# A convolution and gated MLP on one core: output product in 256-column tasks, another order of first products, convolution items also in odd steps' outputs

## Chip, cores, metric

One core of one Trainium2 chip. The metric is the device time of one execution in microseconds, median of several runs; the kernel before takes 2473.99 us (three runs, 2473.96 to 2475.25). "TensorE" is the matmul engine (PE in the profile, PEld for its weight loads), "DVE" is VectorE, "ACT" is ScalarE.

## The reference

```python
# x (8, 4096, 192), weight (8, 7), w_in (192, 2048), w_out (2048, 192), all float32
w = softmax(weight, axis=-1)                       # per head, 7 taps
x_pad = concatenate([zeros((8, 6, 192)), x], axis=1)
conv[b, s, h, :] = sum_k w[h, k] * x_pad[b, s + k, h, :]     # 8 heads of 24 channels
t = conv.reshape(32768, 192)
h = t @ w_in                                       # first product
g = h * sigmoid(1.702 * h)
out = g @ w_out                                    # second product
```

## The kernel before

Tokens go through in 64 steps (s = 0 to 63) of 512, and both products of a step are computed as 2x2 block products with seven multiplications each instead of eight (P1 to P7), so that sums and differences of blocks are made on DVE and fewer matmuls are left for TensorE. A step has the first product in two units (`a` and `b`, half of the hidden columns each), then `output`, the second product. Convolution and loads for later tokens are cut into 31 small items per two steps, queued in `todo`; `work(n)` runs n of them at that place of DVE's program. The output part and the steady step:

```python
LANES = [(0, 0, 0, TA, 0), (1, 0, TA, T - TA, 0), (2, 1, T // 2, T // 2, 0),
         (3, 2, T - TA, TA, 0), (1, 1, 0, T // 2, T - TA), (2, 2, 0, T - TA, T // 2)]
# T = 256, TA = 192: three 32-row chunks of 256 tokens dealt to four strips of 192 columns

def product2(slot, bank, a, b, first=True):
    dst = slot[:, bank, 0:TA]
    for j in range(NK):                            # NK = 8 slices of the contraction
        for l, c, t, n, at in LANES:
            nc.tensor.matmul(dst[l * Q : (l + 1) * Q, at : at + n],
                             w_out_s[:, a, j, c * Q : (c + 1) * Q], g[:, b, j, t : t + n], ...)
    return dst

def output(s, last, work):
    ra, rb = last.x, last.z                        # two PSUM buffers of two banks each
    # ... cut: tiles u1, u2, u3, u7, osb
    p1 = product2(ra, 0, A11, B11);  act.copy(u1, p1)
    # ... cut: four sums of g on DVE
    p3 = product2(rb, 0, S4, B22);   act.copy(u7, p3)
    work(2 if s > 1 else None)
    c11 = product2(ra, 0, A12, B21, first=False);  turn(0, 0, c11)
    work(2)
    p6 = product2(rb, 1, S2, T2);    vec.tensor_add(u2, u1, p6)
    work(3)
    p7 = product2(ra, 1, S3, T3)
    p5 = product2(ra, 0, S1, T1)
    # ... cut: three additions, a transpose, an addition, a transpose
    p4 = product2(rb, 0, A22, T4)
    vec.tensor_sub(u3, u3, p4);  turn(1, 0, u3)
    store(s, osb)                                  # 12 DMAs

# ... cut
for s in range(1, N_ST):
    if nxt is None:                                # s = 1 and 2
        a.p1(); a.seed(); a.p5(); a.p5b(); a.p6(); a.keep2()
        a.p2(); a.h11(); a.p7(); a.keep3()
    else:
        a.p6(); a.p5(); a.p5b(); a.keep2(); a.p7(); a.keep3(); a.p2(); a.h11()
    # ... cut
    work(6 if s > 1 else 9)
    a.add22(); a.h22(); a.p4(); a.h21()            # DVE adds, ACT gelu, matmuls, ACT gelu
    b.p1(); b.seed(); a.p3()                       # seed: ACT copies b.x into `sums`
    work(2 if s == 1 else None if s % 2 else 4)
    a.add12(); b.p5(); b.p6()                      # p6 adds into `sums`, after seed
    # ... cut
    output(s, b, work)
    if s % 2 and (s + 3) // 2 < N_BIG:
        todo += prepare((s + 3) // 2)
```

p5 and p5b write `a.z`, which is the buffer `ra` of the output just before.

Of the kernel before, what the change touches and what calls it, by code (L numbers as in the profile page):

```python
# [8 lines left out]
F32 = mybir.dt.float32  # L9
# [6 lines left out]
def kernel(  # L16
# [27 lines left out]
    nc = tc.nc  # L44
# [5 lines left out]
    P = 128  # L50
    R = 64
    Q = 32
    NC = D // R
    HF = F // 2
    HD = D // 2
    T = 256
    TA = 3 * T // 4
    TOK = 2 * T
    NF = F // P
    NK = NF // 2  # L60
    PAD = K - 1
    CHUNKS = S // TOK
    N_BIG = (B // 2) * CHUNKS
    N_ST = 2 * N_BIG
# [4 lines left out]
    XW = D - Q  # L69
    assert B % 2 == 0 and NC == 3 and D == NC * R and HD == 3 * Q and S % TOK == 0  # L70
    assert UW == 2 * P and PAD <= Q and F % (2 * P) == 0


    LANES = [
        (0, 0, 0, TA, 0),
        (1, 0, TA, T - TA, 0),
        (2, 1, T // 2, T // 2, 0),
        (3, 2, T - TA, TA, 0),
        (1, 1, 0, T // 2, T - TA),
        (2, 2, 0, T - TA, T // 2),  # L80
    ]

    x_v = x.rearrange("(h p) s d -> h p s d", h=2)
    out_v = out.rearrange("(h p s) d -> h p s d", h=2, p=B // 2)
# [44 lines left out]
    T3 = B12  # L129
# [17 lines left out]
    S3 = A21  # L147
# [330 lines left out]
            dst, a, b = [(T1, B12, B11), (T2, B22, T1), (T3, B22, B12), (T4, T2, B21)][i]  # L478
            vec.tensor_sub(v[dst], v[a], v[b])  # L479

    def product2(slot, bank, a, b, first=True):
        dst = slot[:, bank, 0:TA]
        for j in range(NK):

            for l, c, t, n, at in LANES:
                nc.tensor.matmul(  # L486
                    dst[l * Q : (l + 1) * Q, at : at + n],
                    w_out_s[:, a, j, c * Q : (c + 1) * Q],
                    g[:, b, j, t : t + n],
                    start=(first and j == 0 and at == 0),  # L490
                    stop=(j == NK - 1),
                    skip_group_check=True,
                )
        return dst

    def output(s, last, work):

        ra, rb = last.x, last.z
        ut = u_pool.tile([P, 4, TA], F32, name="u")
        osb = osb_pool.tile([P, 2, TA // Q, 2 * Q], F32, name="osb")  # L500
        u1, u2, u3, u7 = (ut[:, i, :] for i in range(4))

        def turn(m, n, src):
            vec.transpose(  # L504
                osb[:, n, :, m * Q : (m + 1) * Q],
                src.rearrange("p (j t) -> p j t", t=Q),
            )

        p1 = product2(ra, 0, A11, B11)
        act.copy(u1, p1)  # L510
        for i in range(4):
            last.sum_g(i)
        p3 = product2(rb, 0, S4, B22)
        act.copy(u7, p3)  # L514
        work(2 if s > 1 else None)
        c11 = product2(ra, 0, A12, B21, first=False)
        turn(0, 0, c11)
        work(2)
        p6 = product2(rb, 1, S2, T2)
        vec.tensor_add(u2, u1, p6)  # L520
        work(3)
        p7 = product2(ra, 1, S3, T3)
        p5 = product2(ra, 0, S1, T1)
        vec.tensor_add(u3, u2, p7)  # L524
        vec.tensor_add(u1, u3, p5)
        vec.tensor_add(u2, u2, p5)
        turn(1, 1, u1)
        vec.tensor_add(u2, u2, u7)
        turn(0, 1, u2)
        p4 = product2(rb, 0, A22, T4)  # L530
        vec.tensor_sub(u3, u3, p4)  # L531
        turn(1, 0, u3)

        store(s, osb)

    def store(s, osb):
        big, odd = divmod(s, 2)
        p, c = divmod(big, CHUNKS)
        t = c * TOK + odd * T
        for n in (1, 0):  # L540
            rows = out_v[n, p, t : t + T, :].rearrange("(j i) (c e) -> c i j e", i=Q, e=2 * Q)
            for i, (l, c, t0, nt, at) in enumerate(LANES):

                (act if i % 2 and s == N_ST - 1 else nc.sync).dma_start(
                    out=rows[c, :, t0 // Q : (t0 + nt) // Q, :],
                    in_=osb[l * Q : (l + 1) * Q, n, at // Q : (at + nt) // Q, :],
                )

    todo = []

    def work(n=None):
        for _ in range(len(todo) if n is None else min(n, len(todo))):
            todo.pop(0)()
# [22 lines left out]
    def first_step():  # L576

        new_f(0)
        for c in (1, 0, 2):
            transpose_x(0, c)  # L580
        first_conv(1)
        first_conv(2)
        xs = xin_pool.tile([P, 2, NJ, XW], F32, name="xin")
        sets[2] = scratch(xs.rearrange("p n j d -> p (n j d)"))

        for k in range(3):
            conv(0, 0, k)
        split_piece(0)
        split_rest(0)
        for k in range(3, K):  # L590
            conv(0, 0, k)
        cross(0, C11, C21, nc.gpsimd)
        split_piece(1)
        split_rest(1)
        take_conv(1)
        round_w_in(0)
        load_w_out(0)
        split_piece(2)
        split_rest(2)
        take_conv(2)  # L600
        round_w_in(1)
        load_w_out(1)
        split_piece(3)
        split_rest(3)


        quarters = [
            (0, 0, slots[0], B11), (0, 1, sums, B12), (1, 0, slots[1], B21), (1, 1, slots[2], B22)
        ]
        w = ((W11, W12, W13), (W21, W22, W23))  # L610
        x = ((C11, C12), (C21, C22), (C31, C32))
        units = [Unit(0, u) for u in range(NU)]

        for m, n, slot, b in quarters:
            for k in range(2):
                units[0].pe(slot, w[m][k], x[k][n], k == 0)
        for m, n, slot, b in quarters:
            units[0].pe(slot, w[m][2], x[2][n])
            units[0].gelu(b, slot)
        round_w_in(2)  # L620
        load_w_out(2)
        split_piece(4)
        split_rest(4)
        round_w_in(3)
        load_w_out(3)
        load_x(1)
        split_piece(5)
        split_rest(5)
        sums_w_in(0)
        round_w_out(0)  # L630
        round_w_out(1)
        split_piece(6)
        split_piece(7)
        for m, n, slot, b in quarters:
            for k in range(3):
                units[1].pe(slot, w[m][k], x[k][n], k == 0)
            units[1].gelu(b, slot)
        split_rest(6)
        split_rest(7)
        round_w_out(2)  # L640
        round_w_out(3)
        sums_w_in(1)
        for i in range(4):
            sums_c(0, i)
        cross(0, C12, C21)
        cross(0, V1, NB)


        todo.extend(prepare(1))
        osb = osb_pool.tile([P, 2, TA // Q, 2 * Q], F32, name="osb")  # L650
        for k in range(2):
            for m in range(2):
                for n in range(2):
                    src = product2(
                        slots[1 - n],
                        m,
                        (A11, A12, A21, A22)[2 * m + k],
                        (B11, B12, B21, B22)[2 * k + n],
                        first=(k == 0),
                    )  # L660
                    if k == 1:
                        work((5, 0, 1, 3)[2 * m + n])
                        vec.transpose(
                            osb[:, n, :, m * Q : (m + 1) * Q],
                            src.rearrange("p (j t) -> p j t", t=Q),
                        )
                        if n == m == 0:
                            sums_w_out()
        store(0, osb)

    first_step()
    nxt = None
    for s in range(1, N_ST):
        a, b = nxt or Unit(s, 0), Unit(s, 1)
        if nxt is None:
            a.p1()
            a.seed()
            a.p5()
            a.p5b()
            a.p6()  # L680
            a.keep2()
            a.p2()
            a.h11()
            a.p7()
            a.keep3()
        else:
            a.p6()
            a.p5()
            a.p5b()
            a.keep2()  # L690
            a.p7()
            a.keep3()
            a.p2()
            a.h11()
        nxt = Unit(s + 1, 0) if s + 1 < N_ST and s != 1 else None
        work(6 if s > 1 else 9)
        a.add22()
        a.h22()
        a.p4()
        a.h21()  # L700
        b.p1()
        b.seed()
        a.p3()
        work(2 if s == 1 else None if s % 2 else 4)
        a.add12()
        b.p5()
        b.p6()
        b.keep2()
        a.h12()
        b.p2()  # L710
        b.p7()
        b.keep3()
        b.h11()
        if nxt:
            nxt.p1()
        b.p5b()
        work(2)
        a.sum_g(0)
        a.sum_g(1)
        b.add22()  # L720
        b.p4()
        b.h21()
        b.h22()
        if nxt:
            nxt.seed()
        b.p3()
        a.sum_g(2)
        a.sum_g(3)
        b.add12()
        b.h12()  # L730
        if s == 1:
            work(1)
        output(s, b, work)
        if s % 2 and (s + 3) // 2 < N_BIG:
            todo += prepare((s + 3) // 2)


# [28 lines left out]
```

## Time and profile before

| | kernel before |
|---|---|
| median time | 2473.99 us |
| span of the profiled run | 2474.9 us |
| PE, DVE, ACT busy | 99%, 69%, 38% |
| a steady step | 37.80 us: second product 18.61, first 19.20 |

In a list of groups, the columns are line, engine, operation, output and inputs, count, then busy time, mean ns of one, and idle time with what ended it.

### The profile page before, as it was taken

The page shows a single profiled execution, that of the slowest core. Times are in us where ns is not written, and L with a number is a line of the kernel's source. Part 1 is how long each engine was busy: PE and PEld are TensorE (multiplying, and loading weights), DVE is VectorE, ACT ScalarE, POOL GpSimd, SP SyncE. Part 2 cuts the span into 40 slices and gives each one's busy share as a digit, 9 for nine tenths or more (in the row PEclk, how much of TensorE's full clock was granted, in tenths as well). Part 3 has the DMA queues.
Part 4 walks back from the last instruction along what each step waited for, and adds up shares of the span by engine and source line. Part 5 has one row for each costly group of instructions (what it writes and reads, how often), then busy time and mean ns, then how long its engine had stood idle before and what let it go on. Part 6 is the DMA issues. An engine that isn't in the chain of part 4 may idle for free.

```text
span 2474.9 us, 114517 instructions
## 1 busy us (share of the span) xinstructions
PE 2454.8 (99%) x54434; PEld 2281.6 (92%) x54434; DVE 1701.4 (69%) x2348; ACT 941.2 (38%) x1052; POOL 8.1 (0%) x27
## 2 busy tenths in 40 slices
PE   9899999999999999999999999999999999999999
PEld 7799999999999999999999999999999999999998
DVE  8677666676666766666766667666676666677654
ACT  5333343343433433433434334334343343343342
POOL 1000000000000000000000000000000000000000
PEclk9999999999999999999999999999999999999999
DMA  7312122121221221221212212222122122121110
GB/s 178 66 37 59 36 56 58 29 57 40 52 58 32 56 55 37 58 46 40 58 40 53 58 32 55 47 45 57 37 50 58 36 56 50 37 58 40 28 35 16
DMA packets 197732, 123.58 MB, mean 50 GB/s; under 512 B 116048, under 2 KB 191440, under 8 KB 193296
## 3 DMA queue, kind: packets, MB, share of 16 engines
q1 hardware_dynamic: 196224, 115.32, 22.2%
q8 instruction: 425, 6.96, 1.2%
q0 software_dynamic: 288, 0.79, 0.1%
q14 instruction: 43, 0.35, 0.0%
q10 hardware_dynamic: 752, 0.16, 0.0%
HBM read 53.15 MB, written 25.17 MB: 32 GB/s over the span
## 4 chain that ended last, share of the span: by engine, by line
PE 98%; DVE 1%; issue 0%; DMA 0%; ACT 0%; SPq 0%; ACTq 0%; DVEq 0%
PE slot L486 49%; PE slot L390 31%; PE sums L390 18%; DMA f<-f 0%; DMA xin<-in_x_dram 0%; ACT g L413 0%; DVE f L353 0%; SPq L114 0%; DVE g L479 0%; DVE u L460 0%; DVE xt L336 0%; ACT u L430 0%; ACT u L443 0%; DVE osb L504 0%; DVE f L221 0%
## 5 line engine op out<-in xcount | busy, mean ns | idle before, releaser
L486 PEld LDWEIGHTS slot<-g,w_out_s 128*32 128x32 f32 x43104 | 1190.3, 110 | 35.2 <-issue 33.8
L486 PE MATMUL slot<-g,w_out_s 128*32 128x128 f32 (+2 forms) x43104 | 1208.2, 273 | 7.2 <-issue 6.1
L390 PE MATMUL slot<-f,w_in_s 64*128 64x256 f32 x7200 | 843.7, 376 | 0.4 <-DMA f<-f 0.2
L390 PEld LDWEIGHTS slot<-f,w_in_s 64*128 64x128 f32 x7200 | 692.8, 187 | 88.2 <-DVE u L460 1.8
L479 DVE TENSOR_TENSOR g<-g 128x1024 f32<-128x1024 f32 x504 | 600.2, 1222 | 191.5 <-ACT g L413 187.2
L390 PE MATMUL sums<-f,w_in_s 64*128 64x256 f32 x4080 | 511.9, 379 | 2.8 <-ACT u L443 2.8
L430 ACT COPY u<-sums 128x1024 f32<-128x1024 f32 x126 | 127.5, 1012 | 1004.6 <-PE sums L390 1004.6
L390 PEld LDWEIGHTS sums<-f,w_in_s 64*128 64x128 f32 x4080 | 390.4, 187 | 53.2 <-ACT u L443 4.4
L353 DVE SCALAR_TENSOR_TENSOR f<-xt,cw,f 128x512 f32<-128x512 f32 x564 | 421.9, 748 | 14.4
L413 ACT ACTIVATE g<-u 128x1024 f32<-128x1024 f32 x252 | 265.6, 1054 | 17.1 <-DVE u L470 14.4
L470 DVE TENSOR_TENSOR u<-u,slot 128x1024 f32<-128x1024 f32 x126 | 153.4, 1217 | 69.7 <-PE slot L390 69.7
L524 DVE TENSOR_TENSOR u<-u,slot 128x192 f32<-128x192 f32 x63 | 22.3, 354 | 247.6 <-PE slot L486 247.6
L460 DVE TENSOR_TENSOR u<-u,slot 128x1024 f32<-128x1024 f32 x126 | 153.2, 1216 | 54.2 <-ACT u L443 54.0
L443 ACT COPY u<-sums 128x1024 f32<-128x1024 f32 x126 | 127.5, 1012 | 128.4 <-PE sums L390 128.4
L413 ACT ACTIVATE g<-sums 128x1024 f32<-128x1024 f32 x128 | 130.4, 1019 | 94.7 <-PE sums L390 94.7
L413 ACT ACTIVATE g<-slot 128x1024 f32<-128x1024 f32 x132 | 135.4, 1027 | 49.8 <-PE slot L390 49.8
L423 ACT COPY sums<-slot 128x1024 f32<-128x1024 f32 x126 | 126.8, 1006 | 41.7 <-PE slot L390 39.7
L520 DVE TENSOR_TENSOR u<-u,slot 128x192 f32<-128x192 f32 x63 | 22.3, 354 | 93.2 <-PE slot L486 93.2
L514 ACT COPY u<-slot 128x192 f32<-128x192 f32 x63 | 20.1, 319 | 144.8 <-PE slot L486 144.8
L504 DVE STREAM_TRANSPOSE osb<-u 128x192 f32<-128x192 f32 x189 | 71.1, 376 | 4.3
L336 DVE STREAM_TRANSPOSE xt<-xin 128x576 f32<-128x576 f32 x96 | 67.1, 750 | 1.4 <-DMA xin<-in_x_dram 1.3
L531 DVE TENSOR_TENSOR u<-u,slot 128x192 f32<-128x192 f32 x63 | 22.3, 354 | 48.8 <-PE slot L486 48.8
(78 smaller groups left out, 317.1 us busy)
## 6 DMA issues: line engine op xcount, KB each, us to landing
xin<-in_x_dram SPq DMA_DIRECT2D x240, 180.0 KB, 4.3
f<-f SPq DMA_DIRECT2D x62, 576.0 KB, 4.8
out_dram<-osb SPq DMA_DIRECT2D x254, 48.0 KB, 1.7
out_dram<-osb SPq DMA_DIRECT2D x256, 32.0 KB, 1.6
out_dram<-osb SPq DMA_DIRECT2D x252, 16.0 KB, 1.5
g<-in_moe_w_in_dram SPq DMA_DIRECT2D x8, 384.0 KB, 9.2
g<-in_moe_w_out_dram SPq DMA_DIRECT2D x4, 768.0 KB, 5.2
xin<-in_x_dram SPq DMA_DIRECT2D x16, 160.0 KB, 3.0
```

Of the source, the lines that this page charges most:

```text
L336: vec.transpose(xts[big][:, c, :, :].rearrange("p n (j t) -> p (n j) t", t=Q), xins[big].rearrange("p n j d -> p (n j) d")[:, :, c * R : c ...
L353: vec.scalar_tensor_tensor(out=dst, in0=src, scalar=tap, in1=dst, op0=ALU.mult, op1=ALU.add)
L390: nc.tensor.matmul(slot[:, h, j * T : (j + 1) * T], w_in_s[halves[h], u, a, j * P : (j + 1) * P], f[halves[h], 0 if h == o else 1, b, :], ...
L413: act.activation(g[:, b, j : j + NK // NU, :].rearrange("p f t -> p (f t)"), src.rearrange("p h n -> p (h n)"), AF.Gelu_apprx_sigmoid,)
L423: act.copy(sums, self.x)
L430: act.copy(self.u2, sums)
L443: act.copy(self.u3, sums)
L460: vec.tensor_add(self.u3, self.u3, self.z)
L470: vec.tensor_add(self.u2, self.u2, self.z)
L479: vec.tensor_sub(v[dst], v[a], v[b])
L486: nc.tensor.matmul(dst[l * Q : (l + 1) * Q, at : at + n], w_out_s[:, a, j, c * Q : (c + 1) * Q], g[:, b, j, t : t + n], start=(first and j ...
L504: vec.transpose(osb[:, n, :, m * Q : (m + 1) * Q], src.rearrange("p (j t) -> p j t", t=Q),)
```

## The change

Its intent is to run the second product in matmuls of 256 columns on all four strips, at half the number of instructions. The fourth strip takes a chunk of P3 or P4 beside three chunks of another product; the last chunk of P4 is split over the four strips (`quarters`), two slices each: ACT copies one of the four partial sums out and DVE adds the other three. P7 is now the last task, so P2 and P7 of the next first product go ahead of P5, which needs P7's buffer. DVE has more to do in the output, so convolution items are spread over odd outputs as well.

```diff
-    def product2(slot, bank, a, b, first=True):
+    def product2(slot, bank, ab, last, first=True):
+        dst = slot[:, bank, 0:T]
+        tiles = [(c, *ab, c) for c in range(NC)] + [(NC, *last)]
         for j in range(NK):
-            for l, c, t, n, at in LANES:
+            for l, a, b, c in tiles:
                 nc.tensor.matmul(
-                    dst[l * Q : (l + 1) * Q, at : at + n],
+                    dst[l * Q : (l + 1) * Q, :],
                     w_out_s[:, a, j, c * Q : (c + 1) * Q],
-                    g[:, b, j, t : t + n],
+                    g[:, b, j, :],
  ... (cut: quarters, Out.turn and Out.store, the first step)
     def output(s, last, work):
+        p1, p3c = product2(ra, 0, (A11, B11), (S4, B22, 0))
         act.copy(u1, p1)
+        act.copy(chunk(p3, 0), p3c)
  ... (cut: sums of g)
+        p2, p3c = product2(rb, 0, (A12, B21), (S4, B22, 1))
+        act.copy(chunk(p3, 1), p3c)
         work(2)
+        vec.tensor_add(u2, u1, p2)
+        out.turn(0, 0, u2)
+        work(2)
+        p6, p3c = product2(ra, 1, (S2, T2), (S4, B22, 2))
+        act.copy(chunk(p3, 2), p3c)
         vec.tensor_add(u2, u1, p6)
         work(3)
+        p5, p4c = product2(rb, 1, (S1, T1), (A22, T4, 0))
+        q = quarters(rb, 0, A22, T4, 2)
+        act.copy(chunk(p4, 0), p4c)
+        vec.tensor_add(u1, u2, p5)
+        act.copy(chunk(p4, 2), q[2])
+        vec.tensor_add(p3, u1, p3)
+        out.turn(0, 1, p3)
+        for l in (0, 1, 3):
+            vec.tensor_add(chunk(p4, 2), chunk(p4, 2), q[l])
+        work(3)
+        p7, p4c = product2(ra, 0, (S3, T3), (A22, T4, 1))
+        act.copy(chunk(p4, 1), p4c)
+        vec.tensor_add(u1, u1, p7)
+        vec.tensor_add(u2, u2, p7)
+        out.turn(1, 1, u1)
+        vec.tensor_sub(u2, u2, p4)
+        out.turn(1, 0, u2)
+        out.store()                                # 6 DMAs
  ... (cut: the lines that these replace)
             a.p7()
+            b.p1()                                 # s = 1 and 2
             a.keep3()
         else:
             a.p6()
+            a.keep2()
+            a.p2()
+            a.h11()
+            a.p7()
+            a.keep3()
             a.p5()
             a.p5b()
-            a.keep2()
-            a.p7()
-            a.keep3()
-            a.p2()
-            a.h11()
-        work(6 if s > 1 else 9)
+        work(4 if s > 1 else 9)
-        b.p1()
+        if s > 2:
+            b.p1()
-        work(2 if s == 1 else None if s % 2 else 4)
+        work(None if s % 2 and s > 1 else 2)
  ... (cut: work(2) becomes work(1) ahead of unit a's sums of g)
-        output(s, b, work)
         if s % 2 and (s + 3) // 2 < N_BIG:
             todo += prepare((s + 3) // 2)
+        output(s, b, work)
```

More of the change, by code (lines that the diff above doesn't have):

```diff
@@ L56 @@
     T = 256
-    TA = 3 * T // 4
     TOK = 2 * T
@@ L71 @@
     assert UW == 2 * P and PAD <= Q and F % (2 * P) == 0
-    LANES = [
-        (0, 0, 0, TA, 0),
-        (1, 0, TA, T - TA, 0),
-        (2, 1, T // 2, T // 2, 0),
-        (3, 2, T - TA, TA, 0),
-        (1, 1, 0, T // 2, T - TA),
-        (2, 2, 0, T - TA, T // 2),
-    ]
     x_v = x.rearrange("(h p) s d -> h p s d", h=2)
@@ L479, in sum_g @@
             vec.tensor_sub(v[dst], v[a], v[b])
-    def product2(slot, bank, a, b, first=True):
-        dst = slot[:, bank, 0:TA]
+    def product2(slot, bank, ab, last, first=True):
+        dst = slot[:, bank, 0:T]
+        tiles = [(c, *ab, c) for c in range(NC)] + [(NC, *last)]
         for j in range(NK):
-            for l, c, t, n, at in LANES:
+            for l, a, b, c in tiles:
                 nc.tensor.matmul(
-                    dst[l * Q : (l + 1) * Q, at : at + n],
+                    dst[l * Q : (l + 1) * Q, :],
                     w_out_s[:, a, j, c * Q : (c + 1) * Q],
-                    g[:, b, j, t : t + n],
-                    start=(first and j == 0 and at == 0),
+                    g[:, b, j, :],
+                    start=(first and j == 0),
                     stop=(j == NK - 1),
@@ L493, in product2, with quarters @@
                 )
-        return dst
+        return dst[0 : NC * Q, :], dst[NC * Q :, :]
+    def quarters(slot, bank, a, b, c):
+        dst = [slot[l * Q : (l + 1) * Q, bank, 0:T] for l in range(4)]
+        for i in range(NK // 4):
+            for l in range(4):
+                j = NK // 4 * l + i
+                nc.tensor.matmul(
+                    dst[l],
+                    w_out_s[:, a, j, c * Q : (c + 1) * Q],
+                    g[:, b, j, :],
+                    start=(i == 0),
+                    stop=(i == NK // 4 - 1),
+                    skip_group_check=True,
+                )
+        return dst
@@ new lines, with __init__, turn, store @@
+    class Out:
+        def __init__(self, s):
+            self.s = s
+            self.osb = osb_pool.tile([NC * Q, 2, T // Q, 2 * Q], F32, name="osb")
+        def turn(self, m, n, src):
+            vec.transpose(
+                self.osb[:, n, :, m * Q : (m + 1) * Q],
+                src.rearrange("p (j t) -> p j t", t=Q),
+            )
+        def store(self):
+            big, odd = divmod(self.s, 2)
+            p, c = divmod(big, CHUNKS)
+            t = c * TOK + odd * T
+            for n in (1, 0):
+                rows = out_v[n, p, t : t + T, :].rearrange(
+                    "(j i) (c e) -> c i j e", i=Q, e=2 * Q
+                )
+                for c in range(NC):
+                    (act if c % 2 and self.s == N_ST - 1 else nc.sync).dma_start(
+                        out=rows[c], in_=self.osb[c * Q : (c + 1) * Q, n, :, :]
+                    )
@@ L496, in output, with chunk @@
+    def chunk(t, c):
+        return t[c * Q : (c + 1) * Q, :]
     def output(s, last, work):
         ra, rb = last.x, last.z
-        ut = u_pool.tile([P, 4, TA], F32, name="u")
-        osb = osb_pool.tile([P, 2, TA // Q, 2 * Q], F32, name="osb")
-        u1, u2, u3, u7 = (ut[:, i, :] for i in range(4))
-        def turn(m, n, src):
-            vec.transpose(
-                osb[:, n, :, m * Q : (m + 1) * Q],
-                src.rearrange("p (j t) -> p j t", t=Q),
-            )
-        p1 = product2(ra, 0, A11, B11)
+        out = Out(s)
+        u1, u2, p3, p4 = (
+            u_pool.tile([NC * Q, T], F32, name=f"u{i}") for i in range(4)
+        )
+        p1, p3c = product2(ra, 0, (A11, B11), (S4, B22, 0))
@@ L510, in output @@
         act.copy(u1, p1)
+        act.copy(chunk(p3, 0), p3c)
         for i in range(4):
             last.sum_g(i)
-        p3 = product2(rb, 0, S4, B22)
-        act.copy(u7, p3)
-        work(2 if s > 1 else None)
-        c11 = product2(ra, 0, A12, B21, first=False)
-        turn(0, 0, c11)
-        work(2)
-        p6 = product2(rb, 1, S2, T2)
+        p2, p3c = product2(rb, 0, (A12, B21), (S4, B22, 1))
+        act.copy(chunk(p3, 1), p3c)
+        work(2)
+        vec.tensor_add(u2, u1, p2)
@@ L520, in output @@
+        out.turn(0, 0, u2)
+        work(2)
+        p6, p3c = product2(ra, 1, (S2, T2), (S4, B22, 2))
+        act.copy(chunk(p3, 2), p3c)
         vec.tensor_add(u2, u1, p6)
         work(3)
-        p7 = product2(ra, 1, S3, T3)
-        p5 = product2(ra, 0, S1, T1)
-        vec.tensor_add(u3, u2, p7)
-        vec.tensor_add(u1, u3, p5)
-        vec.tensor_add(u2, u2, p5)
-        turn(1, 1, u1)
-        vec.tensor_add(u2, u2, u7)
-        turn(0, 1, u2)
-        p4 = product2(rb, 0, A22, T4)
@@ L531, in output @@
-        vec.tensor_sub(u3, u3, p4)
-        turn(1, 0, u3)
-        store(s, osb)
-    def store(s, osb):
-        big, odd = divmod(s, 2)
-        p, c = divmod(big, CHUNKS)
-        t = c * TOK + odd * T
-        for n in (1, 0):
-            rows = out_v[n, p, t : t + T, :].rearrange("(j i) (c e) -> c i j e", i=Q, e=2 * Q)
-            for i, (l, c, t0, nt, at) in enumerate(LANES):
-                (act if i % 2 and s == N_ST - 1 else nc.sync).dma_start(
-                    out=rows[c, :, t0 // Q : (t0 + nt) // Q, :],
-                    in_=osb[l * Q : (l + 1) * Q, n, at // Q : (at + nt) // Q, :],
-                )
+        p5, p4c = product2(rb, 1, (S1, T1), (A22, T4, 0))
@@ L649, in first_step @@
         todo.extend(prepare(1))
-        osb = osb_pool.tile([P, 2, TA // Q, 2 * Q], F32, name="osb")
+        out = Out(0)
+        c22 = u_pool.tile([NC * Q, T], F32, name="u0")
+        quarter = [(0, 0), (0, 1), (1, 0)]
         for k in range(2):
-            for m in range(2):
-                for n in range(2):
-                    src = product2(
-                        slots[1 - n],
-                        m,
-                        (A11, A12, A21, A22)[2 * m + k],
-                        (B11, B12, B21, B22)[2 * k + n],
-                        first=(k == 0),
-                    )
-                    if k == 1:
-                        work((5, 0, 1, 3)[2 * m + n])
-                        vec.transpose(
-                            osb[:, n, :, m * Q : (m + 1) * Q],
-                            src.rearrange("p (j t) -> p j t", t=Q),
-                        )
-                        if n == m == 0:
-                            sums_w_out()
-        store(0, osb)
+            for i, (m, n) in enumerate(quarter):
+                c, c22c = product2(
+                    slots[i % 2],
+                    i // 2,
+                    ((A11, A12, A21, A22)[2 * m + k], (B11, B12, B21, B22)[2 * k + n]),
+                    ((A21, A22)[k], (B12, B22)[k], i),
+                    first=(k == 0),
+                )
+                if k == 1:
+                    work((6, 1, 3)[i])
+                    out.turn(m, n, c)
+                    act.copy(chunk(c22, i), c22c)
+                    if i == 0:
+                        sums_w_out()
+        out.turn(1, 1, c22)
+        out.store()
     first_step()
@@ L716 @@
         b.p5b()
-        work(2)
+        work(1 if s > 1 else 2)
         a.sum_g(0)
```

## The prediction

> **What bounds the kernel now.** I read the busy shares first, then the chain that ended last, then the waits, then single stretches of the timeline. The page's first part and its DMA queue part:
>
> ```profile
> PE 2454.8 (99%) x54434; PEld 2281.6 (92%) x54434; DVE 1701.4 (69%) x2348; ACT 941.2 (38%) x1052; POOL 8.1 (0%) x27
> ...
> q8 instruction: 425, 6.96, 1.2%
> ```
>
> TensorE is busy for 99% of the span at a granted clock of 0.999, and nothing else is near. DVE has 31% in hand, ACT 62%. The q8 row counts instruction fetches: 425 blocks in 6.96 MB, so 16 KB each. TensorE has 54434 matmul and 54434 weight-load records, 108868 / 425 = 256 per block, so q8 is in effect TensorE's instruction stream.
>
> The chain that ended last, over two steady steps (start us, duration us, what):
>
> ```profile
> 1034.94 3.45 PE slot L390 x32
> ...
> 1045.30 1.73 PE slot L390 x16
> 1047.03 18.61 PE slot L486 x338
> 1065.63 1.06 PE sums L390 x8
> 1066.70 1.73 PE slot L390 x16
> ...
> 1084.83 18.61 PE slot L486 x338
> ```
>
> The chain is TensorE alone. A step is 1084.83 - 1047.03 = 37.80 us: 18.61 us of the second product (L486) and 19.19 us of the first (L390). So a change to the output code pays only through the 18.61 us, or through a wait that it puts in or takes out. Now the second product by tile form:
>
> ```profile
> L486 PE MATMUL slot<-g,w_out_s 128*32 128x128 f32 x14368 | 1204.7, 273 | 3.1 <-issue 3.0
> L486 PE MATMUL slot<-g,w_out_s 128*32 128x192 f32 x14368 | 1202.6, 327 | 2.0 <-issue 1.2 <-DVE osb L504 0.7
> L486 PE MATMUL slot<-g,w_out_s 128*32 128x64 f32 x14368 | 1201.7, 219 | 2.1 <-issue 2.0
> L486 PEld LDWEIGHTS slot<-g,w_out_s 128*32 128x32 f32 x43104 | 1190.3, 110 | 35.2 <-issue 33.8
> ```
>
> Each matmul leaves two records (21552 are in the program, 43104 here). Six matmuls per k-slice run on four 32-column strips of the array, a third each of 192, 128 and 64 columns; each strip streams 192 columns. What it waits for, and one stretch of the timeline:
>
> ```profile
> PE slot L486 <- issue: 6.1, 12, 2.3
> PE sums L390 <- ACT u L443: 2.8, 4, 1.2
> PE slot L486 <- DVE osb L504: 0.7, 1, 0.7
> ```
>
> ```profile
> 187.99 3.77 PE L486 MATMUL slot<-g,w_out_s 128*32 128x64 f32 x128 [0.20 <-issue]
> 187.99 3.46 PEld L486 LDWEIGHTS slot<-g,w_out_s 128*32 128x32 f32 x128 [0.35 <-issue]
> ...
> 191.99 0.74 PE L486 MATMUL slot<-g,w_out_s 128*32 128x192 f32 x17 [0.24 <-issue]
> 191.99 0.47 PEld L486 LDWEIGHTS slot<-g,w_out_s 128*32 128x32 f32 x16 [0.54 <-issue]
> ```
>
> Between two halts lie exactly 128 matmuls and 128 weight loads, 256 instructions, one fetched block. The halts are the instruction stream running dry: a block is used up in about 3.5 us here and the next came after 4.0 us. Of the 61 step lengths from the second steady step on, about 40 are 37.8 us; the others are 0.05 to 1.2 us longer, all of it inside L486.
>
> **What the Trainium skill says.** (1) "TensorE: Matmul & The Clock Gate", Back-to-back issue gap: one column per cycle at 2.4 GHz plus about 2.5 ns per matmul. Here a record takes two cycles per column: the first product's 32 records of 256 columns, two row halves at once, take 3.45 us, 3.45 / 16 = 215.6 ns = 512 / 2.4 + 2.3. It agrees. (2) "Runtime: NRT & Kernel Launch", Instruction fetch mechanics: TensorE's instructions come in blocks of 16 KB, 256 instructions, by the sequencer's own DMA queue, and the cost is mostly hidden. The block size agrees exactly; hidden it is not, as just shown. (3) "TensorEngine Tiling (Array Packing)", Tiling Modes: changing the tiling mode drains TensorE. The first piece after L486 is 1.06 us where others of 8 records take 0.86, so 0.2 us; the change keeps both switches of a step.
>
> **The change, part by part.**
>
> *Shape.* A second product is now a task of four strips of 256 columns: three chunks of one product and, on the fourth strip, one chunk of P3 or P4. Five tasks of 8 k-slices and the two rounds of the quartered P4 chunk make 42 rounds. Streaming is unchanged: 56 x 192 = 42 x 256 = 10752 columns per strip. Only the fixed cost moves. Before, the busiest strips take four records per k-slice (64, 64, 128, 128): 384 x 2 / 2.4 + 4 x 2.5 = 330 ns, and 56 of them make 18.48 us (the chain's 18.61 holds the switch too). After, two records of 256 columns per round, 2 x 215.8 = 431.6 ns, times 42 = 18.13 us. Gain 0.35 us, i.e. 140 record overheads of 2.5 ns. Solving for the overhead with the chain's numbers alone (384c + 4r = 18610 / 56 = 332.3 and 256c + r = 215.6) gives r = 3.3 ns and 0.47 us; I take 0.36. Over 63 steps: **22.7 us**. The first step (64 slices of 330 ns against 48 of 431.6) gives 0.4.
>
> *Instructions.* L486 goes from 43104 matmul records to 63 x 336 + 384 = 21552, with as many weight loads. A round issues 16 instructions in 431.6 ns, 37 per us, where a k-slice issued 24 in 330 ns, 73 per us. A block lasts 6.9 us instead of 3.5, against a supply that took about 4. The fetch halts should go. Their size: PEld waited 33.8 us for "issue" in 91 waits at L486; about 63 are the mode switch at 0.33 us (20.8), which leaves 13.0. Gaps between starts of L486's matmuls in the trace, less their normal spacing and the one DVE wait, add up to 11.6 us, 2.4 of it in the first step and 4 in step 1. Gain **11 us**.
>
> *Step 1 and 2.* b.p1 moves ahead of the p4 that waits for keep3; that wait (1.16 us in each of the two steps, in the sums line above) is filled with 0.86 us of work, **1.7 us** in both. The 0.8 us wait of step 1 for the transpose of c11 goes, since P1 is now copied out and P2 has a bank of its own: **0.8 us**.
>
> *DVE.* Now six adds of about 0.35 and four transposes of 0.376, 3.6 us a step. After: seven adds of 96x256, three of 32x256 and four transposes of 256. An add of 256 columns takes 0.422 (row L360), a transpose about 0.438 (0.376 at 192 columns and 0.750 at 576 give 0.97 ns a column): 10 x 0.422 + 4 x 0.438 = 6.0 us. 2.4 us more a step, 150 in all, DVE at about 75%: beside TensorE, so no cost unless late.
>
> *ACT.* Two copies of 0.32 become seven of about 0.37 (0.32 at 192 and 1.01 at 1024 columns), 2.0 us more a step, 43% in all: hidden.
>
> *Tail.* After the last matmul came one subtraction, one transpose and the last stores. Now two adds, a transpose, a subtraction and a transpose, about 2.15 us against 0.75, but three stores per half instead of six. Loss about **0.8 us**. Step 3 has a backlog of seven items ahead of its cross transfer and may wait some 0.5 us for it.
>
> Sum: 22.7 + 0.4 + 11 + 1.7 + 0.8 - 0.8 - 0.5 = 35.3 us, 2474.0 - 35.3 = 2438.7; I say **2438.5 us**, 1.4% less.
>
> **The rivals.**
>
> *P7's late reads become a wait.* P7 is last and DVE reads it twice (u1, u2) before that slot may be written again by p5 of the next step. From the start of the output: PE ends at 18.13 us. DVE ends the four sums of g at 7.3 us (as before), then items, adds and transposes; three convolutions precede the P7 adds, which I put at 18.7 to 19.5 us. With P2 and P7 of the first product moved ahead, p5 starts after 0.2 + 0.86 + 1.73 + 0.86, at 21.8 us: 2.3 us of slack. Without that reordering p5 would start at 19.2 and wait. Next, add22 must end before a.p3 at 26.1: DVE is free at about 23.5 in the worst (even) steps, add22 ends at 24.75. And p4 waits for keep3 (ACT, about 23.0) and starts at 23.5: slack 0.5 us, the narrowest. If I am wrong there by 0.3 us a step, 19 us go and the time is about 2457.
>
> *The fetch halts stay.* If they come from fetch latency after each burst and not from rate, some of the 11 us stays: 2444 to 2450. Against it: the block count in between is exactly one, and the first product, at 18.5 instructions per us, has none.
>
> *Fixed costs are larger than I think.* With r = 3.3 ns the gain grows by 7 us, 2432. A cut of over 2% needs 49.5 us; streaming is untouched, so I see no source for it.
>
> *Fewer, larger stores* (6 instead of 12 a step) are hidden anyway, worth nothing: the DMA engines are a tenth to a fifth busy.
>
> **Range and chances.** The two solid terms, 22 and 11 us, have errors of some +7/-3 and -6; waits of the first rival weigh on the slow side. Range 2431 to 2450. Faster by over 2% 0.03, within 2% 0.95, slower by over 2% 0.02.
>
> **What would show it.** L486 (then another line) with 21552 matmul records, all of 256 columns, in chain pieces of about 18.25 us; steps of 37.45 us, all alike; q8 at 257 blocks (65764 / 256); "issue" waits of PEld near 21 us; DVE near 1850 us busy, ACT near 1065; no wait of PE for DVE or ACT in steady steps. Wrong would be: steps that alternate between two lengths with PE waiting on DVE or ACT at p5, p4 or a.p3; a round that takes over 440 ns; or issue gaps that remain.

## More of the kernel before

Of the chain that ended last (followed back from the last instruction, share of the span by engine) the page says:

```profile
PE 98%; DVE 1%; issue 0%; DMA 0%; ACT 0%; SPq 0%; ACTq 0%; DVEq 0%
```

"PE 98%" says that TensorE almost never waited.

## The result, and the profile after

The changed kernel takes 2455.76 us (four runs, 2455.66 to 2457.46) against 2474.01 us of before (four runs). The ratio is 0.9927, interval 0.9909 to 0.9944. The change is faster by 18 us, 0.7%, about half of the 35.5 us forecast, and outside the range.

From the page of the changed kernel: busy shares, the instruction queue, the chain by engine, and the second product's matmuls.

```profile
PE 2434.3 (99%) x32882; PEld 1780.8 (73%) x32882; DVE 1837.9 (75%) x2600; ACT 1064.9 (43%) x1370; POOL 7.5 (0%) x27
...
q8 instruction: 257, 4.21, 0.7%
...
PE 80%; DVE 13%; ACT 4%; issue 2%; DMA 0%; SPq 0%; DVEq 0%; ACTq 0%
...
L476 PE MATMUL slot<-g,w_out_s 128*32 128x256 f32 x20544 | 1133.3, 379 | 0.0
```

Counts and loads came out as predicted: 20544 records here and the rest of the 21552 in `quarters`, 257 blocks, DVE 1838 us, ACT 1065 us, and no idle time ahead of these matmuls. The line that did not is the chain: 80% TensorE where it was 98%, with 13% DVE and 4% ACT. The PE busy share of 99% hides this, as matmul records overlap the short waits.

Two steps of that chain in order of time (start us, duration us, what). The first one shown is an odd step's output with the even step's first product behind it:

```profile
997.30 13.95 PE slot L476 x256
1011.25 0.91 PE slot L492 x16
1012.18 0.38 ACT u L557
1012.58 0.43 DVE u L558
...
1017.65 0.42 DVE u L567
...
1022.06 1.23 DVE u L449
1023.60 0.67 issue
1024.27 1.02 ACT g L402
1025.31 1.01 ACT sums L412
1026.36 1.14 PE sums L379 x8
...
1035.27 13.95 PE slot L476 x256
1049.22 0.86 PE slot L492 x16
1050.08 3.45 PE slot L476 x64
1053.54 1.06 PE sums L379 x8
```

From 1012 to 1026 us the chain has left TensorE. It runs from the end of the quarters (L492) through a copy of ACT (L557, the first chunk of P4), DVE's addition of P5 (L558), its additions of P7 (L567), add22 (L449), two gelus (the chain counts most of the first as "issue"), the seed (L412), to the second unit's p6. In the next step, from 1035 us on, it is TensorE alone. The starts of the matmuls in the trace give the same picture for all steps: the second product takes 18.27 us in every steady step (18.61 before). The first takes 19.20 us in odd steps and **19.70 us in even steps from 4 to 60**, against 19.20 in all steps from 3 on before, but for two steps 0.3 us longer.

The waits of the changed kernel (who waited for whom, total us, times, longest; the last line is TensorE's weight loads):

```profile
ACT u L557 <- PE slot L492: 248.8, 63, 4.0
DVE u L558 <- ACT u L557: 142.7, 63, 3.9
PE sums L379 <- ACT sums L412: 5.3, 31, 0.2
PE slot L379 <- DVE u L568: 1.7, 1, 1.7
PEld sums L379 <- ACT sums L412: 17.7, 31, 0.6
```

The first two are the start of the detour, in all 63 steps. The third is its end: 31 times p6 waited for the seed. It shows 5.3 us only, as the modelled end of the matmul before reaches into the wait; the weight loads of the same p6 waited 17.7 us. By the starts, each even step loses 0.5 us: 0.4 up to p6's start, 0.06 of it at a.p3, and 0.1 in p6's first matmuls. The fourth is one wait in step 2, for the second addition of P7.

Where the time went, from the starts of all tasks in the two profiled runs (spans 2474.9 and 2454.0 us, 20.8 apart, the terms rounded; the profiled run of before is 2.7 us above its median):

| | forecast | measured |
|---|---|---|
| second product, streaming and fixed cost | -23.1 | -22.1 |
| second product, halts and the wait of step 1 | -11.8 | -17.0 |
| first product, even steps from 4 on | 0 | +14.9 |
| first product, steps 1 to 3 | -1.2 | +2.8 |
| first product, two halts of before | 0 | -0.6 |
| start and tail | +0.8 | +1.1 |
| sum | -35.3 | -20.9 |

### The profile page after: what moved, and what is told of

It reads as the page before. It is cut to its first block, busy times and chain, and to the rows that moved or that the text cites. A ratio compares the mean times of both kernels' runs of the same rounds, so it can differ in the third digit from the quotient of the medians.

```text
span 2454.0 us, 71535 instructions
## 1 busy us (share of the span) xinstructions
PE 2434.3 (99%) x32882; PEld 1780.8 (73%) x32882; DVE 1837.9 (75%) x2600; ACT 1064.9 (43%) x1370; POOL 7.5 (0%) x27
## 4 chain that ended last, share of the span: by engine, by line
PE 80%; DVE 13%; ACT 4%; issue 2%; DMA 0%; SPq 0%; DVEq 0%; ACTq 0%
PE slot L476 41%; PE slot L379 23%; PE sums L379 14%; DVE f L342 5%; PE slot L492 2%; ACT g L402 2%; DVE u L449 2%; DVE osb L510 2%; DVE u L563 2%; ACT sums L412 1%; DVE u L560 1%; DVE u L567 1%; DVE u L558 1%; PE slot L587 1%; DVE f L340 1%
## 5 line engine op out<-in xcount | busy, mean ns | idle before, releaser
L476 PE MATMUL slot<-g,w_out_s 128*32 128x256 f32 x20544 | 1133.3, 379 | 0.0
L476 PEld LDWEIGHTS slot<-g,w_out_s 128*32 128x32 f32 x20544 | 661.1, 110 | 451.1 <-issue 21.2
L449 DVE TENSOR_TENSOR u<-u,slot 128x1024 f32<-128x1024 f32 x126 | 153.2, 1216 | 38.0 <-PE slot L379 33.6
L432 ACT COPY u<-sums 128x1024 f32<-128x1024 f32 x126 | 127.3, 1010 | 35.3 <-PE sums L379 35.3
L558 DVE TENSOR_TENSOR u<-u,slot 96x256 f32<-96x256 f32 x63 | 26.3, 417 | 142.7 <-ACT u L557 142.7
L557 ACT COPY u<-slot 32x256 f32<-32x256 f32 x63 | 23.2, 368 | 248.8 <-PE slot L492 248.8
L412 ACT COPY sums<-slot 128x1024 f32<-128x1024 f32 x126 | 126.9, 1007 | 2.9 <-PE slot L379 0.7
L510 DVE STREAM_TRANSPOSE osb<-u 96x256 f32<-96x256 f32 x253 | 111.1, 439 | 6.9 <-ACT u L690 0.4
L552 ACT COPY u<-slot 32x256 f32<-32x256 f32 x63 | 23.1, 367 | 194.3 <-PE slot L476 194.3
L546 ACT COPY u<-slot 32x256 f32<-32x256 f32 x63 | 23.2, 369 | 170.3 <-PE slot L476 170.3
L566 ACT COPY u<-slot 32x256 f32<-32x256 f32 x63 | 23.2, 368 | 141.0 <-PE slot L476 141.0
```

What stands on the lines that cost most here:

```text
L412: act.copy(sums, self.x)
L432: act.copy(self.u3, sums)
L449: vec.tensor_add(self.u3, self.u3, self.z)
L476: nc.tensor.matmul(dst[l * Q : (l + 1) * Q, :], w_out_s[:, a, j, c * Q : (c + 1) * Q], g[:, b, j, :], start=(first and j == 0), stop=(j == ...
L510: vec.transpose(self.osb[:, n, :, m * Q : (m + 1) * Q], src.rearrange("p (j t) -> p j t", t=Q),)
L558: vec.tensor_add(u1, u2, p5)
```

## The experiments

**Theory 1** says that DVE is late in even steps. Its addition of P5 starts about 1.3 us after P5 is done, because it waits for a copy by ACT which waits for the quarters. All that follows on DVE is later, up to add22, and from there the delay goes through ACT to p6. **Theory 2** is that ACT is late by itself (seven copies instead of two). **Theory 3** is that the new place of p5 and p5b leaves p4 and p3 too little room. Each experiment below is the changed kernel with the edit shown. All were correct. The stretches quoted (first product of a step, second product) are again distances between starts of matmuls.

### e1: copy and addition ahead of the quarters

```diff
-        q = quarters(rb, 0, A22, T4, 2)
         act.copy(chunk(p4, 0), p4c)
         vec.tensor_add(u1, u2, p5)
+        q = quarters(rb, 0, A22, T4, 2)
```

> The copy of P4's first chunk and the addition of P5 are placed ahead of the quartered chunk's matmuls; nothing else differs from the changed kernel. Theory 1 (the lost time is that DVE reaches add22 late in even steps, because its addition of P5 waits for a copy that itself waits for the quarters): the copy starts some 0.9 us earlier, the even steps' product 1 falls from 19.70 to 19.20 us, 30 x 0.5 = 15 us less than the changed kernel, 2440 to 2442 us. Theory 2 (ACT is late: its seven copies and the order of gelu 22, gelu 21 and seed) and theory 3 (the new place of p5 and p5b leaves p4 and a.p3 too little room): the even steps stay at 19.70 us, 2454 to 2457 us.

Measured: 2510.44 us, ratio to before 1.0146 (1.0131 to 1.0161). A miss: 55 us slower than the changed kernel. Its waits of TensorE have a new line:

```profile
PE slot L492 <- DVE u L557: 59.0, 63, 0.9
```

L492 are the quarters and L557 is here the addition of P5. The even steps' first product did fall from 19.70 to 19.20 us, as theory 1 has it, though this alone would not show it, since the halt of TensorE told next gives DVE time too. The quarters now wait 0.94 us in each of 63 steps for the addition that stands ahead of them, and the second product takes 19.41 us instead of 18.27 (1.14 more; again the recorded wait is the shorter). They write bank 0 of the buffer, and the addition reads bank 1. So this program orders accesses by the whole two-bank buffer. Accesses to P5 written behind the quarters wait for the quarters; quarters written behind the accesses wait for those. That is where the 0.9 us of L557 came from in the changed kernel.

### e2: two items moved behind add22

```diff
-        work(4 if s > 1 else 9)
+        work((4 if s % 2 else 2) if s > 1 else 9)
         a.add22()
  ...
-        work(None if s % 2 and s > 1 else 2)
+        work(None if s % 2 and s > 1 else 4 if s > 1 else 2)
         a.add12()
```

> Two convolution items (1.5 us of DVE) of the even steps move from before add22 to after it; ACT, the copies and the order on TensorE are untouched. Theory 1 (DVE late at add22): add22 starts 1.4 us earlier or as soon as p5b is done, even steps 19.20 us, about 2440 to 2442 us, as in the experiment with the copy. Theory 2 (ACT) and theory 3 (order of p5): no change, 2454 to 2457 us.

Measured: 2441.25 us, ratio 0.9869 (0.9853 to 0.9885), 14.5 us less than the changed kernel. The even steps' first product is 19.20 us, and in the waits of TensorE the one for the seed is left only twice:

```profile
PE sums L379 <- ACT sums L412: 0.3, 2, 0.2
```

Neither ACT's work nor TensorE's order differs from the changed kernel, so theories 2 and 3 are out. DVE's lateness at add22 cost 14.6 of the 14.9 us; the other 0.27 us are in step 16, which e2 has too, and their cause was not looked for.

### e5: the addition ahead of the copy, both behind the quarters

```diff
         q = quarters(rb, 0, A22, T4, 2)
-        act.copy(chunk(p4, 0), p4c)
         vec.tensor_add(u1, u2, p5)
+        act.copy(chunk(p4, 0), p4c)
```

> Against the changed kernel two lines change places: the addition of P5 (DVE) is written ahead of the copy of P4's first chunk (ACT), both still after the quarters. If DVE's lateness is what costs (theory 1), DVE no longer waits for a 0.37 us copy of the same bank: the addition starts at the end of the quarters, 0.4 us earlier, add22 too, and the 0.5 us of the even steps shrink to about 0.1: 12 us less, 2443 to 2446 us. If only the amount of work or ACT mattered, nothing would change: 2455 us.

Measured: 2443.2 us, ratio 0.9879 (0.9864 to 0.9893). The even steps' first product is 19.30 us. The timeline shows the two instructions (start us, us, engine, operation, idle before and what ended it):

```profile
1007.92 0.42 DVE L557 TENSOR_TENSOR u<-u,slot 96x256 f32<-96x256 f32 x1 [2.32 <-PE slot L492]
1008.37 0.37 ACT L558 COPY u<-slot 32x256 f32<-32x256 f32 x1 [4.40 <-DVE u L557]
```

Now DVE waits for the quarters alone and ACT waits for DVE. So DVE had lost 0.4 us to a copy that reads other partitions of the same bank, and these 0.4 us alone were worth 0.4 us per even step. In the Trainium skill, "PSUM — Partial Sum Buffer", section "PSUM bank collisions raise a hardware error", two engines must not touch one bank in the same quadrant of 32 partitions at once, reads included, while different quadrants are allowed. The copy (partitions 96 to 127) and the addition (0 to 95) are in different quadrants, so this program's waits are stricter than what the page asks. No run here tried without them.

### e8: the quarters behind P7

```diff
-        q = quarters(rb, 0, A22, T4, 2)
-        act.copy(chunk(p4, 0), p4c)
         vec.tensor_add(u1, u2, p5)
+        act.copy(chunk(p4, 0), p4c)
  ... (P3's addition, transpose, work(3))
         p7, p4c = product2(ra, 0, (S3, T3), (A22, T4, 1))
+        q = quarters(rb, 0, A22, T4, 2)
         vec.tensor_add(u1, u1, p7)
         vec.tensor_add(u2, u2, p7)
  ... (both copies of P4, transpose; the three additions of q last)
```

> The quarters are moved behind P7, so that nothing of P4's third chunk stands between P5 and its readers, and P7's additions come ahead of the quarters' additions on DVE. P7 then ends 0.87 us earlier and its additions should end at about the end of TensorE's work instead of 2.9 us after it. Theory 1: even steps 19.20 us without moving any item, and step 2's wait of 1.7 us for P7's second addition goes too: 2437 to 2441 us. If the number of items ahead of add22 alone decides: even steps still above 19.3 us, 2448 to 2456 us.

Measured: 2439.44 us, ratio 0.9863 (0.9848 to 0.9878). All steady steps have 19.20 us for the first product, with every item where the changed kernel has it. The same additions of P7, and the first matmuls of the next step:

```profile
1006.99 0.41 DVE L563 TENSOR_TENSOR u<-u,slot 96x256 f32<-96x256 f32 x1
1007.32 0.41 DVE L564 TENSOR_TENSOR u<-u,slot 96x256 f32<-96x256 f32 x1
...
1007.69 1.14 PE L379 MATMUL sums<-f,w_in_s 64*128 64x256 f32 x8
```

P7 is read by the time TensorE leaves the second product, where the changed kernel ended these additions 2.9 us after it. Step 2's wait is gone too. So neither the items nor the extra work on DVE was too much in itself. The order in which results were handed over made DVE late.

### e3: each 256-column matmul in two halves

```diff
             for l, a, b, c in tiles:
-                nc.tensor.matmul(dst[l * Q : (l + 1) * Q, :], ..., g[:, b, j, :], ...)
+                for h in range(2):
+                    nc.tensor.matmul(dst[l * Q : (l + 1) * Q, h * P : (h + 1) * P], ...,
+                                     g[:, b, j, h * P : (h + 1) * P], ...)
```

> Each 256-column matmul of the five tasks is split into two of 128 columns: the same streaming, twice the instructions (73 per us in these tasks, as in the kernel before). Fixed cost alone: 40 rounds x 2 extra records x 2.5 ns = 0.2 us a step, 13 us, so 2468 to 2470 us if the halts of the kernel before came from its 64-column matmuls. If they came from the instruction stream, halts of 0.1 to 0.6 us between blocks of 256 instructions are back inside the second product, 8 to 25 us more: 2476 to 2494 us, with 425 blocks or so fetched again.

Measured: 2488.0 us (2482.29 to 2489.45), ratio 1.0052 (1.0037 to 1.0067). From its page, the instruction queue and the second product's matmuls:

```profile
q8 instruction: 417, 6.83, 1.2%
...
L477 PE MATMUL slot<-g,w_out_s 128*32 128x128 f32 x41088 | 1171.4, 273 | 6.9 <-issue 6.8
```

No matmul has 64 columns here, and the halts are back. (The profiled run, 2482.29 us, is the fastest of the four; the figures that follow are of it.) A second product without halts takes 18.54 us, and the actual ones go up to 19.80. The sum over all steps is 37 us above the changed kernel's: 17 us are fixed cost (63 x 0.27) and about 20 us are halts. The even steps' wait shrank by some 10 us meanwhile, presumably because a halt of TensorE gives DVE time to catch up. So the halts of the kernel before came with the number of instructions in that time, not with 64-column matmuls.

### e4: p5 back ahead of p7 and p2

```diff
             a.p6()
+            a.p5()
+            a.p5b()
             a.keep2()
-            a.p2()
-            a.h11()
             a.p7()
             a.keep3()
-            a.p5()
-            a.p5b()
+            a.p2()
+            a.h11()
```

> One part of the change undone: in steady steps p5 and p5b come right after p6 again, ahead of p7 and p2. The trace of the changed kernel has p5 ready about 1.06 us after the second product's end, and the second addition of P7 ending 2.9 us after it in even steps and 2.4 us in odd ones, so p5 should wait 1.8 and 1.4 us; the 0.5 us wait of even steps goes. About 1.35 us a step, 80 us in all: 2515 to 2550 us. If this order were worth nothing: 2456 us.

Measured: 2566.54 us, ratio 1.0374 (1.0359 to 1.039). The longest of the waits of TensorE:

```profile
PE slot L379 <- DVE u L568: 100.1, 61, 1.9
```

L568 is the second addition of P7. The waits are the expected ones, 1.6 us a step. The total is 16 us over the range I gave: the first products of even and odd steps are 1.7 us longer than the changed kernel's, not 1.3 and 1.4, and seven even steps lost 1.7 us more (23.06 us). In one of these seven, the view by stretch of time (us, then busy us of PE, PEld, DVE, ACT and POOL, granted clock, DMA share, GB/s) has this for the 8 us from the end of the output on, and for 3.4 us within them:

```profile
1137.00:1145.00 8.00, 6.09 (x42) 5.48 (x40) 6.43 (x12) 1.91 (x3) 0.00 (x0) 0.79 0.24 50
1141.20:1144.60 3.40, 3.40 (x19) 3.21 (x18) 2.36 (x4) 0.13 (x1) 0.00 (x0) 0.50 0.53 113
```

The 0.79 is a mean: after a wait of 1.9 us the granted clock was 0.50 for 3.4 us and 1.00 around them, and half of 3.4 us is the 1.7 us lost. The trace has such a stretch in each of the seven steps; the other even steps wait 1.9 us as well and keep their clock. This order of the first product is needed, worth about 110 us with the rest in place.

### e6: no convolution items in odd outputs

```diff
-        if s % 2 and (s + 3) // 2 < N_BIG:
-            todo += prepare((s + 3) // 2)
         output(s, b, work)
+        if s % 2 and (s + 3) // 2 < N_BIG:
+            todo += prepare((s + 3) // 2)
```

> One part of the change undone: the convolution items are queued after the odd steps' output again, all else as changed. The backlog of about 14 items then falls on the odd steps, 10 of them ahead of add12, so the cross transfer leaves about 3 us later and the next first product waits for it: odd steps 2 to 4 us longer, even steps 0.5 us shorter: 2505 to 2570 us. If the items in odd outputs were worth nothing or did harm only (they are what makes the even steps late): 2440 to 2456 us.

Measured: 2621.34 us, ratio 1.0613 (1.0582 to 1.0644), more than expected. The wait itself is as foreseen, 30 times up to 3 us for the cross transfer; in the waits of TensorE it reads:

```profile
PE slot L379 <- DMA f<-f: 85.5, 30, 3.0
```

Behind it, the view by stretch of time shows a low clock again:

```profile
1125.00:1130.70 5.70, 5.70 (x36) 4.49 (x35) 3.49 (x3) 1.62 (x2) 0.00 (x0) 0.71 0.02 6
1124.90:1128.30 3.40, 3.40 (x20) 2.73 (x18) 1.95 (x2) 0.00 (x0) 0.00 (x0) 0.50 0.06 19
```

The mean of 0.71 over these 5.7 us is again 3.4 us at 0.50 and the rest at full clock. In the trace, 24 of the 30 waits are followed by a granted clock of 0.50, six of them for 3.4 us and 18 for 6.8 us. The Trainium skill, "TensorE: Matmul & The Clock Gate", section "HAM oscillation — how this bites in real kernels", warns of idle gaps of TensorE over about 3.4 us. Here a wait recorded as 2.9 us, 3.3 us from the last start to the next, was mostly enough, and in e4 sometimes one of 1.9 us. The first product of an odd step is 4.1 us longer where the clock stayed full, not 3, and 5.8 or 7.0 us where it was low: the wait and the low clock add up. So the items in odd outputs are needed as well: without them this kernel would lose over 160 us.

### e7 and e9: versions put together

e7 is e2 and e5 together, with step 2's `b.p1` ahead of p6 and p5 behind p7, two items less ahead of step 1's add22, and five items more in step 2. e9 is e8 with a similar evening out of items in steps 1 and 2 (four more in step 2, no other order there):

```diff
-        work(4 if s > 1 else 9)
+        work(7 if s == 1 else 5 if s == 2 else 4)
-        work(None if s % 2 and s > 1 else 2)
+        work(None if s % 2 and s > 1 else 4 if s < 3 else 2)
-        work(1 if s > 1 else 2)
+        work(1 if s > 2 else 2)
```

> The two changes that theory 1 suggests together (items of even steps moved behind add22, addition ahead of copy), and the early steps: in step 2 p5 waits no longer for the additions of P7 (b.p1 goes there instead and p5 behind p7), step 1 has two items less ahead of add22, step 2 takes five more items so that step 3 has no backlog ahead of its cross transfer. 14.5 us as with the items alone, and about 1.6 + 0.3 + 1 us from steps 1 to 3: 2437 to 2440 us. If the early steps hide another wait: 2441 us, as with the items alone.

> The version with the quarters behind P7, with its early steps evened out: two items fewer ahead of step 1's add22, four items more in step 2, so that step 3 queues its cross transfer earlier. The version without this has 0.8 us over in step 1's first product and 1.4 us over in step 3's: 2 us less than its 2439.4, 2436.5 to 2438 us. If those two waits have other causes: 2439 to 2440 us.

Measured: e7 2437.55 us, ratio 0.9857 (0.9842 to 0.9872); e9 2437.51 us, ratio 0.9849 (0.9835 to 0.9862). First products of steps 1, 2 and 3: 21.42, 22.57, 20.97 us in the changed kernel; 20.64, 21.50, 19.20 in e7; 20.94, 20.94, 19.20 in e9. Step 3 is back at 19.20 in both, so its extra was the backlog ahead of the cross transfer. The two are equal within their spread. Either beats both kernels: 36 us under the kernel before, 18 under the change as it came.

## Why the prediction was wrong

Its estimate of 2438.5 us is what the change gives once DVE is not late (2437.5 to 2441 us in e2, e7, e8 and e9). That they lie so close is in part luck: in the profiled runs the halts were worth 5 us more than forecast and the fixed cost 1 us less, and the profiled run of before is itself 2.7 us above its median. The change as it came has a wait that the prediction looked for, under the first rival, and ruled out.

- **The step that failed** is the DVE schedule there: "three convolutions precede the P7 adds, which I put at 18.7 to 19.5 us" and "DVE is free at about 23.5 in the worst (even) steps, add22 ends at 24.75". From the output's start at 997.23, the trace has the P7 additions at 20.4 to 21.2 us, add22 starting at 24.8 and ending at 26.05. The first 1.3 to 1.4 us of that were lost at once: the 18.7, less the five additions, the transpose and the three convolutions that go before (4.8 us, at 0.75 us a convolution), puts DVE's addition of P5 at 13.9 us, P5's end, and it started at 15.35 us, behind the quarters and a copy (e1, e5, e8). Another 0.3 us of add22's delay are not DVE's: where DVE is in time (odd steps, e2), add22 waits for p5b, starts at 23.84 and ends at 25.06. I took the waits from what the data needs, not from what the program orders.
- **A second gap in the same step**: I checked add22 against a.p3 only (26.1 us). The limit that bound is the ACT chain behind it, gelu, gelu, seed, p6. In even steps add22 ends at 25.29 us in e8 and nothing is lost, at 25.65 in e5 and 0.1 us is lost, at 26.05 in the changed kernel and 0.5 us is lost. So the limit was near 25.55 us: the slack over the forecast 24.75 was 0.8 us, not 1.35, and the lateness was 1.3. The lengths did alternate, as the prediction's signs of being wrong have it, but the place was none of the three named there, bar some 0.06 us at a.p3.
- **"Narrowest slack" at p4** (keep3) was the wrong place: no steady step shows a wait there.
- **Fixed cost per matmul** was right: 18.61 to 18.27 us, 0.34 us forecast as 0.36. The other value given there is miscalculated: its two equations have r = 3.6 ns and 0.50 us, not 3.3 and 0.47.
- **Halts of the instruction stream**: cause right (e3), size too small. I summed the gaps between starts, 11.6 us; the second products of before were 17.0 us longer than their clean length, 0.8 of it the wait in step 1. Of the 17.0, 1.7 us are low clock: in step 1, after a halt recorded as 2.3 us, the granted clock was 0.51 for 3.4 us. The first step and step 1 lost about what I had summed (2.4 and 4.4 us); the steps after them lost 9.4 us where my sum has 5.2, and why it came out low, the record doesn't show. And not all of the longer steps lay in L486: two first products were 0.3 us longer.
- **Steps 1 to 3**: wrong in sign. The fill of keep3's wait by b.p1 worked (2.8 us of waits before, 1.1 after), but steps 1 and 2 were not given the new order of p5, so step 2 waited 1.7 us for P7's second addition, by the very mechanism that the change avoids elsewhere. Step 3's backlog cost 1.8 us, not 0.5.
- **Tail, DVE and ACT loads** were right: 1.1 us forecast as 0.8, 1838 and 1065 us.

The chance given to "within 2%" was right, but the range was too narrow on the slow side. I had priced this rival at 0.3 us a step, 19 us, and kept it out of the range. That its 2457 us is near the measured 2455.76 is luck: it was priced for a wait at p4 in every step, and what came was 0.5 us at p6 in every other step and some 4 us in steps 1 to 3, partly made up by the larger halts saved.

What stays open: whether the waits between bank 0 and bank 1 of a buffer, or between different partitions of a bank, could be left out safely. They belong to the program's ordering, and no experiment removed them.

## What to carry to other kernels

When work moves between engines that share a buffer, write down each reader's start from the waits as they are built, in program order and per buffer, not from when its own data is ready; an accumulation placed between a result and its reader delayed that reader here by 0.9 us. Follow a late instruction past its next user to the matmul that ends the detour, as the slack there is the smallest of all along the way. And where half the instructions stream the same columns, the instruction supply can matter nearly as much as the fixed cost (16 and 22 us here).

## What the Trainium skill lacked or had wrong

- "Runtime: NRT & Kernel Launch", Instruction fetch mechanics: the cost of a block is called mostly hidden. At 73 instructions per us in the second product it was not: about 16 us of halts in the kernel before (1.7 of it low clock), about 20 us in e3, none at 37 per us in the changed kernel. The page gives no supply rate; in second products with halts, fetches of blocks of 256 mostly began 3.4 to 4.3 us apart, where 256 instructions last 3.5 us.
- "TensorE: Matmul & The Clock Gate", Back-to-back issue gap: 2.5 ns per matmul fits the change of shape (0.34 us for 140 records less, 2.4 ns each), but splitting 256 columns into two of 128 cost 0.27 us for 80 records more, 3.4 ns each.
- The same page, HAM oscillation: a gap of about 3.4 us is named as the limit. In e6 24 of 30 waits recorded as 2.2 to 3.0 us (2.54 to 3.35 us from start to start) were followed by a granted clock of 0.50 for 3.4 or 6.8 us, in e4 seven waits of 1.9 us out of some 30 by one of 3.4 us, and in the kernel before one halt of 2.3 us.
- "PSUM — Partial Sum Buffer", PSUM bank collisions: the page says what must be kept apart, but not that a program's own ordering can be coarser. Here a matmul into bank 0 waited 0.94 us for a reader of bank 1 of the same buffer (e1), and in the changed kernel a DVE reader waited 0.4 us for an ACT reader of other partitions (taken away in e5).
